# Padding the rows of a scratch array in a long convolution with spectral mixing, with its stores split by partitions

## The chip, the cores and the metric

The kernel runs on one core of a Trainium2 chip. A core has a matrix engine (PE, whose weight loads are listed apart as PEld), a vector engine (DVE), a scalar engine (ACT), a general engine (POOL) and SyncE (SP), which here only issues transfers. Transfers run on 16 DMA engines that all issuing queues share. The metric is the device time in microseconds (us) of one execution. The kernel before took 372.04 us as the median of three runs (370.41 to 372.57).

## The reference

`x` has 8 batches of 5,696 positions and 128 channels. Two stages follow one another: a causal convolution along the positions with a filter `h` as long as the sequence, by an FFT of twice the length, and a spectral mix of the first 64 modes with a small dense layer behind it.

```python
Xf = np.fft.rfft(x, n=2 * S, axis=1)
Hf = np.fft.rfft(h, n=2 * S, axis=0)
x = np.fft.irfft(Xf * Hf[None], n=2 * S, axis=1)[:, :S, :]
X = np.fft.rfft(x, axis=1)
Y[:, :64] = X[:, :64] @ (w_r + 1j * w_i)          # one 128x128 matrix per mode
u = x + np.fft.irfft(Y, n=S, axis=1)
out = u + np.maximum(u @ w_ch, 0.0)
```

The result must have the reference's shape and type (float32); inside, the kernel works in float16 with float32 sums.

## The kernel before

**The tiling.** 5,696 is 64 x 89. The FFT is done by matrix multiplications in two steps, over the 89 and over the 64; there are 90 coarse frequencies `k` (`NK`), and for each of them 64 fine ones, with real and imaginary part. Two batches go through together, as one group; there are four groups, 0 to 3. A group has 23 ticks (`NT`), each with four of the 90 frequencies, the last with two.

**One tick.** PE makes the spectrum of the tick's frequencies (`second`). ACT or DVE reads it from PSUM, and DVE multiplies it with the filter's spectrum (`products`, line 652) into a tile U. The filter's spectrum `h_sb` has two halves: `Hs` as it is cast from PSUM, and a copy with the partitions 0 to 63 and 64 to 127 exchanged. That exchange is made by two DMA copies of 64 partitions, issued by SP (`filter_tick`), once per tick and only while group 0 runs: the first six ticks' copies before the ticks begin, and then tick t makes those of tick t + 6. Two ticks later (`LC` = 2) PE transforms U back over the 64 fine frequencies with the matrices W1 and W2, and ACT casts the two results from PSUM into one of the tiles Zs and Zt (6 of them in the first ticks, later 8 or 10). One tick after that `modes` reads the same tile, to sum the 64 modes that the mix needs.

**Z and its scratch array.** Z doesn't fit into SBUF with all the rest, so each tick stores its tile to the array `zscr` in HBM: partition p = ri x 64 + j (ri is the real or imaginary part, j the position within the 64) with four frequencies of 2 x 128 channels each, 512 bytes in a piece. In the array a row is one (frequency, ri) and holds the 64 j one after the other, 64 x 512 = 32,768 bytes. In the last stage `load_zt` reads chunks of 16 j: 128 rows into one tile (ZT0a to ZT4a) and the remaining 52 into another (ZT0b to ZT4b), 8,192 bytes from each row. Sixteen chunks are read; the first ones begin during the ticks of group 3. PE then finishes the inverse transform from them (`u_z`), adds the mixed modes (`u_c`), and does the dense layer (`o_tile`), whose results SP stores to the output.

**The order of the work.** Everything is put in order by hand. `Recorder` notes each operation with what it reads and writes, and adds semaphore waits; each engine then runs its own list in that order. All DMAs on the SP list are issued one after the other: one that waits, or is slow to issue, holds up those behind it. In tick t of group 0 the list has the Z store of tick t - 2, then the two Hs copies of tick t + 6, and after every other tick up to 11 a load of the table G. Each DMA takes the next semaphore of its ring (`z` for Z stores, 10 of them; `s` for Hs copies, 8), and before a semaphore is used again its former DMA must have landed. The ring `q` has no user.

POOL issues the loads of x for the next group (two DMAs at a time) and of the mix weights. Nearly all operations are recorded by helpers, so the profile names lines of helpers: 320 issues a DMA, 323 a matmul, 311 and 313 are ACT's reads of PSUM, 315 and 317 DVE's.

Of the kernel before, what the change touches and what calls it, by code (L numbers as in the profile page):

```python
# [4 lines left out]
P = 128  # L5
F16 = mybir.dt.float16
# [117 lines left out]
def bass_long_conv_fft__then__afno_spectral_mix_kernel(nc, x, h, moe_w_r, moe_w_i, moe_w_ch, out):  # L124
    B, S, D = x.shape
    M = moe_w_r.shape[0]
    assert D == P and M == 64 and B == 8
    J = 64
# [3 lines left out]
    NK = NQ + 1  # L132
    NP = B // 2
    KT = 4
    NT = (NK + KT - 1) // KT
# [15 lines left out]
    c, s = np.cos(th), np.sin(th)  # L151
# [43 lines left out]
    c_sg = nc.inline_tensor(np.ascontiguousarray(sg.astype(np.float32)), name="cSG")  # L195
    c_g = const("cG", g)
    wd = nc.dram_tensor("wscr", [P, 2 * M * D], F16, kind="Internal")
    zs = nc.dram_tensor("zscr", [NP * NK * P, 2 * D], F16, kind="Internal")


    base = (nc.sbuf_base + 63) // 64 * 64
# [4 lines left out]
    def at(name, cols, dt, off):  # L206
        return nc.alloc_sbuf_tensor_at(name, [P, cols], dt, offset=off)
# [39 lines left out]
    z_s = [at(f"Zs{i}", 1024, F16, a_st + NU * 4096 + (NXS + i) * 2048) for i in range(NZ)] + \  # L247
# [8 lines left out]
    ZB = 16  # L256
    NC = 5
    ZP = ZB * 2 * D
# [5 lines left out]
    zt = [[at(f"ZT{i}{'ab'[p_]}", ZP, F16, zt_off[i][p_]) for p_ in range(2)] for i in range(NC)]  # L264
# [28 lines left out]
        return bass.AP(ps, p0 * 4096 + bank * 512 + off, [[4096, n]] + [list(d) for d in dims])  # L293

    R = Recorder(nc)
    for name, n in (("c", 16), ("x", 26), ("z", 10), ("w", 16), ("t", 20), ("s", 8), ("o", 12), ("p", 16), ("q", 10)):
        R.ring(name, n)

    def bank(i):
        return ("bank", i)  # L300
# [18 lines left out]
    def dma(eng, dst, src, ring, reads=(), writes=(), after=()):  # L319
        R.add(eng, lambda h_: h_.dma_start(dst, src), reads, writes, ring=ring, after=after)  # L320
# [6 lines left out]
    def once(key, toks):  # L327
        if key in first:
            return []
        first[key] = 1  # L330
        return list(toks)
# [3 lines left out]
    def turns(name, items):  # L335
        i = ring2.get(name, 0)
        ring2[name] = i + 1
        return items[i % len(items)]
# [18 lines left out]
    def x_load(g_, i, dst, toks, after=()):  # L357
        b, c_ = divmod(i, XC)
        for p_, (q0, n) in enumerate(((QA, NQ - QA), (0, QA))):
            dma("gpsimd", bass.AP(dst, q0 * XB, [[XB, n], [1, XB]]),  # L360
                bass.AP(x.tensor, x.offset + (2 * g_ + b) * S * D + q0 * J * D + c_ * XB, [[J * D, n], [1, XB]]),
                "x", (), [toks[p_]], after=after)

    def x_place(i, src, toks):
        R.add("vector", lambda e: e.tensor_copy(bass.AP(x_sb, i * XN * XS, [[XW, NQ], [XS, XN], [1, D]]),  # L365
                                                src),
              list(toks) + XZ, [("xin", i)])
# [73 lines left out]
    for j in range(16):  # L441
        t = turns("h", [0, 2, 4])
# [14 lines left out]
        if j % 2:  # L457
            i = j // 2 % 2 * XC + j // 4
# [23 lines left out]
    def xtok(n):  # L482
        return [("xt", n, p_) for p_ in range(2)]

    def x_room(g_, i):
        if g_ > 1:
            return x_st[i]
        return x_h[i] if i < NXH else x_st[i - NXH]
# [41 lines left out]
    def load_zt(i):  # L530
        g_, c_ = divmod(i, J // ZB)
        for part, (p0, r0, n) in enumerate(((0, 0, P), (PB, P, RB))):
            old = list(once(("zt", i % NC, part), zt_old[i % NC][part]))
            dma("sync", bass.AP(zt[i % NC][part], p0 * ZP, [[ZP, n], [1, ZP]]),
                bass.AP(zs, (g_ * 2 * NK + r0) * J * 256 + c_ * ZB * 256, [[J * 256, n], [1, ZP]]),
                "t", [("zd", g_, s_) for s_ in range(NT)], [("zt", i % NC, part)], after=old)

    def clear_zt(i):
        z32 = zt[i][1][0:PB, :].bitcast(U32)
# [44 lines left out]
    def with_h_at(g_, t):  # L584
        return g_ == 0 and t + LH < NT
# [3 lines left out]
    def copied(g_, t, sl):  # L589
        n = len(ticks[t])  # L590
        e = onchip[(g_, t)] = turns("e", list(range(NXS)))
        evac(bass.AP(x_s[e], 0, [[1024, P], [512, 2], [1, n * D]]), pv(sl, 0, [[512, 2], [1, n * D]]), [bank(sl), bank(sl + 1)],
             [("xs", e)], eng="scalar")
        return e

    def twin(g_, t):
        return g_ > 0 and t % 2 == 1

    def straight(g_, t):
        return g_ > 0 and t % 4 == 3  # L600

    def slot_of(g_, t):
        if t == 0:
            return ZSLOT
        if g_ == 0:
            return XSLOT[(t + 1) % 2 if not with_h_at(g_, t) else 0]
        return XSLOT[t % 4 // 2]

    def second(g_, t, d0=0, d1=D, bs=(0, 1)):
        sl = slot_of(g_, t)  # L610
        rd = AST if d1 == D else [("as", j) for j in range(d1 // 4)]
        for i, k in enumerate(ticks[t]):
            for r in range(2):
                for b in bs:
                    col = k * 3 * J + (J if r == 0 else 0) + b * J
                    mm(pv(sl + b, i * D + d0, [[1, d1 - d0]]),
                       ap(m_sb, MW, J * b, J, col, [[1, P]]),
                       ap(a_sb, AW, J * b, J, (2 * k + r) * D + d0, [[1, d1 - d0]]), r == 0, r == 1,
                       rd + mtok(k), [bank(sl + b)])

    def first_u(b, s_, row, tok, d0, d1):
        n = len(ticks[0])
        R.add("vector", lambda e: e.tensor_tensor(  # L623
            bass.AP(u_s[0], b * 512 + d0, [[2048, P], [1024, 2], [D, n], [1, d1 - d0]]),
            bass.AP(s_[0], s_[1] + d0, [[row, P], [0, 2], [D, n], [1, d1 - d0]]),
            bass.AP(h_sb, d0, [[2 * HW, P], [HW, 2], [D, n], [1, d1 - d0]]), MULT),
              [tok, ("h", 0, 0), ("h", 0, 1, 0), ("h", 0, 1, J)], [("u", 0)])
# [36 lines left out]
    def tick(g_, t):  # L664
        if g_ + 1 < NP:
            for i in range(2 * XC):
                if t == XPLACE[g_ > 0][i]:
                    x_place(i, bass.AP(x_room(g_ + 1, i), 0, [[XB, NQ], [D, XN], [1, D]]), xtok(i))
        with_h = with_h_at(g_, t)
        if t < NT:  # L670
            of_two = t > 0 and twin(g_, t - 1)
            if not of_two:
                if straight(g_, t):
                    second(g_, t + 1)
                if t:
                    second(g_, t)
                if t == 1:
                    d_ = DA if g_ else DF
                    second(g_, 0, d_, D, (0,))
                    first_u(0, (ps, slot_of(g_, 0) * 512), 4096, bank(slot_of(g_, 0)), d_, D)  # L680
            products(g_, t, slot_of(g_, t))
            if straight(g_, t):
                copied(g_, t + 1, slot_of(g_, t + 1))
            elif twin(g_, t):
                second(g_, t + 1)
        if g_ + 1 < NP:
            i = t // 2 - 1 if t % 2 == 0 else -1
            if g_ == 0:
                i = XLATE.index(t) + NXH if t in XLATE else -1
            if 0 <= i < 2 * XC:  # L690
                x_load(g_ + 1, i, x_room(g_ + 1, i), xtok(i), [("u", t % NU)] + AST)
        if LC <= t < NT + LC:
            s_ = t - LC
            n = len(ticks[s_])
            i, zi = s_ % NU, zroom(g_, s_)
            zb = [turns("z", ZBANK) for b in range(2)]
            for b in range(2):
                for r in range(2):
                    mm(pv(zb[b], 0, [[1, n * D]]), (W1, W2)[r], u_s[i][:, r * 1024 + b * 512:r * 1024 + b * 512 + n * D],
                       r == 0, r == 1, [("u", i), ("wc",)], [bank(zb[b])])  # L700
                evac(bass.AP(z_s[zi], b * D, [[1024, P], [2 * D, n], [1, D]]),
                     pv(zb[b], 0, [[D, n], [1, D]]), [bank(zb[b])], [("zs", zi, b)], eng="scalar",
                     after=once(("zx", zi, b), Z_OLD) if zi >= NZ else ())
                if b == 0:
                    drained(g_, t, 0)
            zo = (g_ * NK + KT * s_) * P * 256
            dma("sync", bass.AP(zs, zo, [[256, P], [P * 256, n], [1, 256]]),
                bass.AP(z_s[zi], 0, [[1024, P], [256, n], [1, 256]]), "z",
                [("zs", zi, 0), ("zs", zi, 1)], [("zd", g_, s_)])
        drained(g_, t, 1)  # L710
        late = g_ + 1 < NP and t in (NT, NT + 1)
        if late and t > NT:
            modes(g_, t - LM - 1)
            drained(g_, t, 2)
        if LM <= t < NT + LM and not (late and t == NT):
            modes(g_, t - LM)
        if with_h:
            filter_tick(t + LH, [2, 3])
# [126 lines left out]
    for hb in range(2):  # L845
        evac(bass.AP(y_sb, hb * 32 * B, [[2 * M * B, P], [B, 32], [M * B, 2], [1, B]]),
             pv(6 + hb, 0, [[2 * B, 32], [B, 2], [1, B]]), [bank(6 + hb)], [("y", hb)], eng="vector" if hb else "scalar",
             after=ZY)
# [66 lines left out]
    for g_ in range(NP):  # L915
        last = g_ == NP - 1
        order = [(c_, b) for b in range(2) for c_ in range(NCH)] if last else [(c_, b) for c_ in range(NCH) for b in range(2)]
        for n, (c_, b) in enumerate(order):
            i = NCH * g_ + c_
# [46 lines left out]
```

## Time and profile before

| what | value |
|---|---|
| median of three runs | 372.04 us |
| lowest and highest run | 370.41 and 372.57 us |
| span of the profiled execution | 370.1 us |
| ticks of group 0 in it (first product to last) | 43.4 to 88.3 us |
| ticks of group 3 and the first ZT loads | 210 to 262 us |
| last stage | from 256 us |
| Z stores | 92 |
| granted PE clock | 1.00 in all stretches up to 355 us |

The profiled execution is the one that a profiler recorded; its times are counted from its first instruction. "x15" is a number of instructions. In a timeline each row has the start, the length and what ran; rows of the same kind that follow one another closely are merged, and idle time in front is given in brackets with what ended it. Tables by stretch give the busy time of each engine (with the number of instructions), the granted clock, the share of time in which the 16 DMA engines were busy (over 1 where packets overlap) and the bytes per second. A DMA row on SP lasts as long as its issue takes; the time to landing, which is given apart, runs from its issue until the data has arrived.

### The profile page before, as it was taken

The page shows a single profiled execution, that of the slowest core. Times are in us where ns is not written, and L with a number is a line of the kernel's source. Part 1 is how long each engine was busy: PE and PEld are TensorE (multiplying, and loading weights), DVE is VectorE, ACT ScalarE, POOL GpSimd, SP SyncE. Part 2 cuts the span into 40 slices and gives each one's busy share as a digit, 9 for nine tenths or more (in the row PEclk, how much of TensorE's full clock was granted, in tenths as well). Part 3 has the DMA queues.
Part 4 walks back from the last instruction along what each step waited for, and adds up shares of the span by engine and source line. Part 5 has one row for each costly group of instructions (what it writes and reads, how often), then busy time and mean ns, then how long its engine had stood idle before and what let it go on. Part 6 is the DMA issues. An engine that isn't in the chain of part 4 may idle for free.

```text
span 370.1 us, 12455 instructions
## 1 busy us (share of the span) xinstructions
PE 354.7 (96%) x5350; PEld 276.5 (75%) x5350; DVE 291.8 (79%) x332; ACT 316.2 (85%) x499; POOL 75.2 (20%) x117
## 2 busy tenths in 40 slices
PE   7999899999999999999999999999999999999994
PEld 7878766667866668866668766668899888888873
DVE  3549899988999999989999988775357777756666
ACT  8559999999999999999999999995467777688885
POOL 8804012100833311823213001151000000000000
PEclk9999999999999999999999999999999999999999
DMA  7999979969999996999996999999999999999878
GB/s 139 209 271 382 249 165 292 232 198 283 93 140 213 263 258 186 132 160 215 263 278 128 171 310 363 342 345 388 381 410 386 413 410 408 418 399 376 326 291 349
DMA packets 87048, 103.94 MB, mean 281 GB/s; under 512 B 22730, under 2 KB 72522, under 8 KB 83438
## 3 DMA queue, kind: packets, MB, share of 16 engines
q1 hardware_dynamic: 64610, 81.33, 62.5%
q0 software_dynamic: 22384, 21.83, 35.4%
q8 instruction: 42, 0.69, 0.7%
q14 instruction: 12, 0.10, 0.1%
HBM read 70.61 MB, written 51.12 MB: 329 GB/s over the span
## 4 chain that ended last, share of the span: by engine, by line
PE 78%; ACT 10%; DMA 7%; DVE 3%; issue 1%; POOL 1%; DVEq 0%; POOLq 0%
PE ps L323 78%; ACT As L313 6%; DMA out_dram<-O 5%; DMA Hin<-in_h_dram 2%; ACT R L898 1%; DVE As L317 1%; ACT Xs L311 1%; DVE U L623 1%; POOL Hin L320 1%; ACT UT L311 1%; DVE O L899 0%; ACT Zs L311 0%; DVE Hp L438 0%; ACT C L313 0%; DVE Hs L315 0%
## 5 line engine op out<-in xcount | busy, mean ns | idle before, releaser
L652 DVE TENSOR_TENSOR U<-Xs,Hs 128x2048 f16<-128x2048 f16 (+1 forms) x72 | 85.8, 1197 | 12.1 <-ACT Xs L311 11.5
L323 PE MATMUL ps<-U,Wc 128*128 128x512 f16 (+1 forms) x368 | 93.8, 376 | 1.4 <-DVE U L623 1.4
L311 ACT CAST Xs<-ps 128x1024 f16<-128x1024 f32 (+1 forms) x76 | 75.0, 995 | 5.8 <-PE ps L323 3.1
L311 ACT CAST Zs<-ps 128x512 f16<-128x512 f32 (+1 forms) x132 | 70.1, 605 | 0.7
L899 DVE TENSOR_TENSOR O<-ps,R 128x512 f32<-128x512 f32 x81 | 52.4, 684 | 21.6 <-ACT R L898 11.4
L898 ACT ACTIVATE R<-ps 128x512 f32<-128x512 f32 (+1 forms) x92 | 50.5, 592 | 8.5 <-PE ps L323 8.4
L317 DVE TENSOR_SCALAR As<-ps 128x720 f16<-128x720 f32 x64 | 53.1, 879 | 4.8 <-PE ps L323 3.3
L323 PE MATMUL ps<-As,M 64*128 64x128 f16 (+3 forms) x1504 | 52.5, 214 | 2.4 <-ACT As L313 1.2
L313 ACT ACTIVATE As<-ps 128x720 f16<-128x720 f32 (+1 forms) x68 | 48.2, 771 | 5.0 <-PE ps L323 4.8
L323 PE MATMUL ps<-F,Xin 128*128 128x180 f16 x512 | 52.1, 249 | 0.1
L323 PE MATMUL ps<-WI,UT 128*128 128x256 f16 x360 | 50.8, 278 | 0.5 <-ACT UT L311 0.4
L311 ACT CAST UT<-ps 128x712 f16<-128x712 f32 x46 | 34.5, 752 | 19.4 <-PE ps L323 18.4
L323 PEld LDWEIGHTS ps<-U,Wc 128*128 128x128 f16 x368 | 29.1, 97 | 28.2 <-DVE U L623 1.9
L323 PEld LDWEIGHTS ps<-F,Xin 128*128 128x128 f16 x512 | 45.2, 155 | 6.7 <-DVE Xin L365 0.9
L323 PEld LDWEIGHTS ps<-As,M 64*128 64x128 f16 x1504 | 42.2, 94 | 8.7 <-ACT Xs L311 1.9
L323 PEld LDWEIGHTS ps<-WI,UT 128*128 128x128 f16 x360 | 38.9, 152 | 3.2 <-issue 1.8
L323 PE MATMUL ps<-IBs,C 128*128 128x356 f16 x128 | 39.2, 314 | 0.8 <-DVE O L899 0.7
L320 POOL DMA_DIRECT2D Xt<-in_x_dram x40 | 21.4, 540 | 76.5 <-PE ps L323 76.0
L323 PEld LDWEIGHTS ps<-G,Zs 128*128 128x128 f16 x512 | 26.1, 96 | 14.1 <-ACT Zs L311 0.2
L652 DVE TENSOR_TENSOR U<-ps,Hs 128x2048 f16<-128x2048 f32 (+1 forms) x16 | 35.5, 2216 | 0.0
L323 PE MATMUL ps<-G,Zs 128*128 128x128 f16 (+2 forms) x512 | 31.9, 192 | 0.1
L311 ACT CAST Zt<-ps 128x512 f16<-128x512 f32 x52 | 29.1, 659 | 0.0
(76 smaller groups left out, 479.4 us busy)
## 6 DMA issues: line engine op xcount, KB each, us to landing
out_dram<-O SPq DMA_DIRECT2D x39, 512.0 KB, 10.5
zscr<-Zs SPq DMA_DIRECT2D x62, 256.0 KB, 6.7
zscr<-Zt SPq DMA_DIRECT2D x26, 256.0 KB, 6.6
Xt<-in_x_dram POOLq DMA_DIRECT2D x20, 320.0 KB, 6.9
W<-wscr SPq DMA_DIRECT2D x4, 1024.0 KB, 8.5
ZT0a<-zscr SPq DMA_DIRECT2D x4, 1024.0 KB, 11.0
M<-cM POOLq DMA_DIRECT2D x5, 720.0 KB, 17.6
ZT1a<-zscr SPq DMA_DIRECT2D x3, 1024.0 KB, 11.1
```

What stands on the lines that cost most here:

```text
L311: R.add(e, lambda h_: h_.copy(dst, src), reads, writes, after=after)
L313: R.add(e, lambda h_: h_.activation(dst, src, COPY, scale=scale), reads, writes, after=after)
L317: R.add(e, lambda h_: h_.tensor_scalar_mul(dst, src, scale), reads, writes, after=after)
L320: R.add(eng, lambda h_: h_.dma_start(dst, src), reads, writes, ring=ring, after=after)
L323: R.add("tensor", lambda h_: h_.matmul(o, l, r, start=st, stop=sp), reads, writes)
L623: R.add("vector", lambda e: e.tensor_tensor(bass.AP(u_s[0], b * 512 + d0, [[2048, P], [1024, 2], [D, n], [1, d1 - d0]]), bass.AP(s_[0], s_ ...
L652: R.add("vector", lambda e: e.tensor_tensor(uv, src, hv, MULT), bk + [("h", t, 0), ("h", t, 1, 0), ("h", t, 1, J)], [("u", i)])
L898: R.add("scalar", lambda e: e.activation(rv, src_r, RELU), bk, [("r", i % NR)], after=once(("r", i % NR), G_ALL + XTT + [("y", 0), ("y", 1 ...
L899: R.add("vector", lambda e: e.tensor_tensor(ov, src_u, rv, ADD), bk + [("r", i % NR)], [key + (h_,)], after=once(key, old))
```

## The change

A row of `zscr` becomes 34,816 bytes long (64 pieces of 512 bytes and 2,048 bytes that nothing uses). As the rows of the real and imaginary part of one frequency no longer follow one another without a gap, a tick's store becomes two DMAs of 64 partitions each, one per ri, with the same 512-byte pieces. The loads read the same bytes at the new pitch and wait for both stores of each tick. The ring `z` grows from 10 to 16 semaphores, the ring `q` shrinks from 10 to 4.

```diff
-    zs = nc.dram_tensor("zscr", [NP * NK * P, 2 * D], F16, kind="Internal")
+    ZRW = J * 2 * D + 1024
+    zs = nc.dram_tensor("zscr", [NP * NK * 2, ZRW], F16, kind="Internal")
...
-    for name, n in (("c", 16), ("x", 26), ("z", 10), ("w", 16), ("t", 20), ("s", 8), ("o", 12), ("p", 16), ("q", 10)):
+    for name, n in (("c", 16), ("x", 26), ("z", 16), ("w", 16), ("t", 20), ("s", 8), ("o", 12), ("p", 16), ("q", 4)):
...
-                bass.AP(zs, (g_ * 2 * NK + r0) * J * 256 + c_ * ZB * 256, [[J * 256, n], [1, ZP]]),
-                "t", [("zd", g_, s_) for s_ in range(NT)], [("zt", i % NC, part)], after=old)
+                bass.AP(zs, (g_ * 2 * NK + r0) * ZRW + c_ * ZP, [[ZRW, n], [1, ZP]]),
+                "t", [("zd", g_, s_, r) for s_ in range(NT) for r in range(2)], [("zt", i % NC, part)], after=old)
...
-            zo = (g_ * NK + KT * s_) * P * 256
-            dma("sync", bass.AP(zs, zo, [[256, P], [P * 256, n], [1, 256]]),
-                bass.AP(z_s[zi], 0, [[1024, P], [256, n], [1, 256]]), "z",
-                [("zs", zi, 0), ("zs", zi, 1)], [("zd", g_, s_)])
+            for ri in range(2):
+                dma("sync", bass.AP(zs, (2 * (g_ * NK + KT * s_) + ri) * ZRW, [[256, J], [2 * ZRW, n], [1, 256]]),
+                    bass.AP(z_s[zi], ri * J * 1024, [[1024, J], [256, n], [1, 256]]), "z",
+                    [("zs", zi, 0), ("zs", zi, 1)], [("zd", g_, s_, ri)])
```

## The prediction

> **What bounds the kernel now.** I read the page first, for the engines and the chain of waits.
>
> ```profile
> span 370.1 us, 12455 instructions
> ...
> PE 354.7 (96%) x5350; PEld 276.5 (75%) x5350; DVE 291.8 (79%) x332; ACT 316.2 (85%) x499; POOL 75.2 (20%) x117
> ...
> PE 78%; ACT 10%; DMA 7%; DVE 3%; issue 1%; POOL 1%; DVEq 0%; POOLq 0%
> ```
>
> PE is busy for 354.7 of 370.1 us, and the chain that ended last is PE for 78%. No Z transfer is named on it. So the change can take away little: at most some of the 15 us in which PE stands, and most of those are the start and the tail. It can add wherever a transfer that PE or DVE needs becomes late. The question is therefore how close each of SP's transfers is to being late. I looked at the tables by stretch, and then at SP's own timeline in the group that runs with the filter (group 0).
>
> ```profile
> 50.00:62.00 12.00, 12.00 (x246) 7.92 (x240) 11.99 (x15) 11.36 (x18) 2.32 (x4) 1.00 0.98 226
> 62.00:74.00 12.00, 12.00 (x258) 8.09 (x257) 11.67 (x15) 11.46 (x18) 2.07 (x4) 1.00 1.06 248
> 74.00:86.00 12.00, 11.99 (x202) 7.66 (x199) 9.84 (x11) 11.83 (x20) 0.00 (x0) 1.00 0.72 206
> ```
>
> Columns: length, busy PE, PEld, DVE, ACT, POOL, clock, DMA share, GB/s. PE loses nothing from 50 to 86 us: every delay there is new time. SP isn't in that table; its timeline is (start, length, what):
>
> ```profile
> 50.31 0.46 SPq L320 DMA_DIRECT2D zscr<-Zs  x1
> ...
> 69.88 2.04 SPq L320 DMA_DIRECT2D Hs<-Hs  x2
> 71.96 0.59 SPq L320 DMA_DIRECT2D zscr<-Zs  x1
> 72.64 1.22 SPq L320 DMA_DIRECT2D Hs<-Hs  x2
> 73.91 0.60 SPq L320 DMA_DIRECT2D zscr<-Zs  x1
> 74.61 1.45 SPq L320 DMA_DIRECT2D Hs<-Hs  x2
> 76.10 1.20 SPq L320 DMA_DIRECT2D zscr<-Zs  x1
> 77.41 1.10 SPq L320 DMA_DIRECT2D Hs<-Hs  x2
> 78.94 0.36 SPq L320 DMA_DIRECT2D zscr<-Zs  x1
> ...
> 80.59 1.91 SPq L320 DMA_DIRECT2D zscr<-Zs  x1
> 82.60 1.11 SPq L320 DMA_DIRECT2D Hs<-Hs  x2
> ...
> 84.44 1.14 SPq L320 DMA_DIRECT2D Hs<-Hs  x2
> 85.62 1.76 SPq L320 DMA_DIRECT2D zscr<-Zs  x3
> 87.42 2.48 SPq L320 DMA_DIRECT2D zscr<-Zt  x4
> ```
>
> Each row begins some 0.1 us after the one above ends. The only real hole is 0.43 us, before 78.94. SP issues without a rest for 35 us: it is **full**, though nothing on the page says so, since SP has no busy row. In each tick it issues one Z store and one pair of Hs copies, and DVE's product needs that pair:
>
> ```profile
> 77.68 0.41 DVE L315 CAST Hs<-ps 128x256 f16<-128x256 f32 x1
> ...
> 78.62 1.21 DVE L652 TENSOR_TENSOR U<-Xs,Hs 128x2048 f16<-128x2048 f16 x1
> ...
> 87.61 0.69 DVE L652 TENSOR_TENSOR U<-Xs,Hs 128x1024 f16<-128x1024 f16 x1 [0.24 <-ACT Xs L311]
> ```
> ```profile
> zscr<-Zs SPq DMA_DIRECT2D x16, 256.0 KB, 5.0
> Hs<-Hs SPq DMA_DIRECT2D x28, 64.0 KB, 5.2
> ...
> Hs<-Hs SPq DMA_DIRECT2D x2, 32.0 KB, 1.9
> ```
>
> The last tick (22) has two frequencies, so its H is cast at 77.68 (128x256), its copies are the pair of 32 KB, and its product is the 128x1024 one at 87.61. H was ready at 78.09, and SP issued the pair at 84.44: SP is 6.35 us behind. The second copy goes out at about 84.44 + 1.14 - 0.60 = 84.98 and lands 1.9 later, at 86.9: 0.7 us before the product. Five ticks earlier (the pair at 72.64, its second copy at about 73.26) the median landing of 5.2 gives 78.5, for the product at 78.62. Nobody waits for Hs today, by less than a microsecond.
>
> **The change part by part.** *The second store.* The 92 Z stores become 184, all on SP, with the same bytes in the same 512-byte pieces. What does one more issue cost? Three whole stores in a row take 1.76 (0.59 each), four take 2.48 (0.62 each), two Hs copies, which also have 64 partitions and only 64 pieces, 1.14 (0.57 each). So an issue in a full queue costs about 0.57 to 0.62 whatever it moves; I take 0.60.
>
> In group 0 tick t issues the Z store of tick t-2 and then the Hs pair of tick t+6. Ahead of the pair of tick 22 stand the stores of ticks 0 to 14: 15 more issues, 15 x 0.60 = 9.0 us. Subtract the 0.7 of slack and the 0.4 hole: 7.9 us late, if all else on SP stays as it is. It may not. From 50.31 to 85.58 SP spends 35.3 us on 15 stores, 15 pairs and two G loads. At 0.59 a store, 1.12 a pair, 0.14 for the gaps of a tick and 0.64 a G load this would be 15 x 1.85 + 1.3 = 29.1. The other 5.8 us, less the 0.4 hole 5.4, are long issues (2.04, 1.20, 1.91). Some fall on POOL's issues of x loads:
>
> ```profile
> 51.52 1.03 POOL L320 DMA_DIRECT2D Xt<-in_x_dram  x2 [19.76 <-PE ps L323]
> ...
> 69.90 1.04 POOL L320 DMA_DIRECT2D Xt<-in_x_dram  x2 [4.95 <-PE ps L323]
> ```
>
> If the long issues only mean that the transfer engines were full (share 0.98 and 1.06), a slower SP would lose them, and the delay is 7.9 - 5.4 = 2.5. If all stay it is 7.9. Two of the longest stand after 74 us, where the share is 0.72, and the x loads stay, so I keep two thirds: **+6.1 us, between 2.5 and 7.9**. The product is late, then DVE, PE behind it and every later group; no stage has idle time to win it back.
>
> *Groups 1 and 2* cost nothing: SP has no Hs copies there, and mostly waits for the data.
>
> ```profile
> SPq L320 <- ACT Zs L311: 33.0, 14, 16.0
> ```
> ```profile
> L320 SPq DMA_DIRECT2D zscr<-Zs x15: 359/360/1582, 106.6 to 143.1; - x15
> ```
>
> 17 us of waiting behind the first store (33.0 less the longest, 16.0) against 23 issues of 0.36 (8.3 us). Without that cover they'd cost the same 0.6 each.
>
> *Group 3* is full again, with the first ZT loads between the stores:
>
> ```profile
> 239.45 1.81 SPq L320 DMA_DIRECT2D zscr<-Zs  x2
> ...
> 251.47 0.66 SPq L320 DMA_DIRECT2D ZT2a<-zscr  x1
> 252.17 2.37 SPq L320 DMA_DIRECT2D ZT2b<-zscr  x1
> ```
> ```profile
> PEld ps L323 <- DMA ZT2b<-zscr: 0.3, 1, 0.3
> ```
> ```profile
> 245.00:262.00 17.00, 16.13 (x324) 13.63 (x322) 9.14 (x10) 10.41 (x16) 4.95 (x5) 1.00 1.04 377
> ```
>
> PE already waits 0.3 us for ZT2b, so this load has no slack. Seven stores (ticks 13 to 19) stand between 239.45 and 251.47: seven more issues at 0.36 to 0.60 are 2.5 to 4.2 us. But the DMA share is 1.04 there and issues last 2.4 us: SP is held by full transfer engines, and an issue added to that costs nothing while they stay full. Bounds 0 and 4.2; I take 1.0.
>
> *The new pitch* could speed up loads and stores. Z loads alone (262 to 275 us) move 408 GB/s:
>
> ```profile
> DMA packets 998, 5.30 MB, mean 408 GB/s; under 512 B 104, under 2 KB 370, under 8 KB 370
> ```
> ```profile
> 280.00:300.00 20.00, 20.00 (x287) 17.88 (x285) 14.88 (x23) 14.56 (x25) 0.00 (x0) 1.00 1.02 407
> ```
>
> With output stores among them (280 to 300 us) it is 407: the old pitch isn't slower than other traffic, and PE is busy for 20.00 of 20. I take 0 for the pitch; bounds -0.6 (the wait of 0.3 for ZT2b, and one more like it) and 0.
>
> The Trainium skill (DMA: Bandwidth & Descriptors, Latency and other measured facts) tells to pad a pitch that is a large power of two: 512 KiB gives 207 GB/s, a padded one 214. By this rule 32 KiB could gain a few per cent of the loads; the row of 408 GB/s leaves little room for it. The same page (Issuing engines are not separate DMA queues) calls the sequencer's time to issue "usually small relative to the DMA itself"; by that the second store would be free and the sum 372.0. The 0.59 of an issue is small beside a landing of 5.0, as it says, but it is SP's 35 full microseconds that count here.
>
> *The rings.* Ring z has 16 slots for two stores a tick, 8 ticks instead of 10. Z buffers are reused after 6 to 10 ticks, so this waits for nothing new; ring q is not used. ACT now has two store semaphores to wait for before it refills a Z buffer; in group 0 they are late by the same SP delay as Hs, not one more.
>
> *Sum.* 6.1 + 0 + 1.0 + 0 = 7.1 us. The profiled execution spans 370.1; the median of the runs is 372.04, 1.9 us above it. 370.1 + 7.1 = 377.2 profiled, **379.1 us** as a median.
>
> **The rivals.** *A, an issue costs by its pieces.* If half a store took half the issue time, two halves would cost SP what one did, Hs would be as early as now, and the median stay at 372.0 (371.4 with the 0.6 of the pitch): not slower. It decides if halves show 0.30 in the full stretch. Against it: a copy of 64 pieces takes 0.57, a store of 512 pieces 0.59.
>
> *B, the long issues go.* SP's stretches vanish, +2.5 in group 0 and 0 in group 3: 374.5. For it: share 1.06 from 62 to 74 us. Against: 1.91 and 1.20 where the share is 0.72.
>
> *C, 64 partitions move slower.* From 107 to 144 us, in group 1, the two DMA queues take, of 16 engines:
>
> ```profile
> q1 hardware_dynamic: 11349, 5.64, 51.8%
> q0 software_dynamic: 1097, 2.93, 49.2%
> ```
>
> The engines are full there, and 51.8% of 37 us are 19.2 us for 23 stores, 0.83 each. If a store in two halves took a quarter more, 0.21 x 23 = 4.8 us in each of groups 1 and 2 would have no room: 379.1 + 9.6 = 388.7. For it: nothing in the trace shows a store of 64 partitions. Against: Hs copies, which have 64, land in 1.9.
>
> *D, the pitch helps more than I see,* in loads, stores and Hs behind them. The gain is capped by PE's stops between the start and the tail:
>
> ```profile
> 42.00:355.00 313.00, 306.97 (x4817) 235.52 (x4818) 256.04 (x288) 275.19 (x447) 55.09 (x79) 1.00 1.00 283
> ```
>
> 6.0 us in all; half of them would give 369. Against: neither Hs nor, but for 0.3 us, a ZT load costs PE anything now.
>
> **How the numbers follow.** My forecast (SP late by 4 to 12 us in all) 0.62, B 0.13, C 0.08, A 0.11, D 0.06. A change within 0.5% (370.2 to 373.9) can't be told from none. Faster: D, 0.06. Same: A, and of B's low end a little: 0.12. Slower: 0.82. The range goes from 373.2 (between A and B) to 386: 2.5 to 7.9 in group 0 with 0 to 4.2 in group 3 give 374.5 to 384.1, and part of C.
>
> **What would show it.** In the changed profile SP should have no holes from 50 to about 92 us, with second halves of about 0.6; DVE's products of ticks 13 to 22 should wait for Hs<-Hs; the product of 128x1024 should start near 94 instead of 87.6; groups 1 and 2 should keep their length; the wait for ZT2b should grow to about 1 us. I am wrong if halves issue in 0.3, if Hs pairs stay as early as now, or if groups 1 and 2 grow.

## The result, and the profile after

| | before | changed |
|---|---|---|
| median of four runs | 371.88 us | 381.77 us |
| lowest and highest run | 370.41 and 372.57 us | 380.28 and 387.2 us |
| ratio | | 1.025, 95% interval 1.0205 to 1.0294 |
| span of the profiled execution | 370.1 us | 378.4 us |

The changed kernel is slower. Its run of 387.2 us counts as a slow one; ratios leave such runs out, here and below, and medians keep them (without it 380.87 us). The profiled execution is the fastest run, 380.28 us. One line was added above the helpers, so lines 311 to 323 and 652 of before are 312 to 324 and 653 now. From the page of the changed kernel, its totals, the chain that ended last, and the Z stores:

```profile
span 378.4 us, 12581 instructions
...
PE 355.9 (94%) x5350; PEld 275.9 (73%) x5350; DVE 291.6 (77%) x332; ACT 316.8 (84%) x499; POOL 75.9 (20%) x117
...
PE 74%; ACT 11%; DMA 6%; DVE 5%; issue 2%; SPq 1%; POOL 1%; DVEq 0%; ACTq 0%; POOLq 0%
...
zscr<-Zs SPq DMA_DIRECT2D x124, 128.0 KB, 5.9
```

PE has the same 5,350 matmuls and is busy 1.2 us more (354.7 before). So nearly all the new time is time in which PE stands. The page doesn't say where; a table of stage lengths does. A group is counted from the start of its first DVE product to the start of its last, the last stage from the first use of a ZT0 tile to the end (us, worked out from the timelines):

| | group 0 | group 1 | group 2 | group 3 | last stage | span |
|---|---|---|---|---|---|---|
| before | 44.19 | 38.35 | 38.37 | 37.71 | 121.26 | 370.06 |
| changed | 54.36 | 38.36 | 38.43 | 37.70 | 119.98 | 378.44 |

Group 0 grew by 10.17 us. Groups 1, 2 and 3 grew by less than 0.1 each. The last stage is 1.28 shorter, and the rest of the span 0.57 shorter. 10.17 + 0.06 - 1.28 - 0.57 = 8.4, the difference of the spans.

The table by stretch of the changed kernel (length, busy PE, PEld, DVE, ACT, POOL with their instructions, clock, DMA share, GB/s) covers group 0, four of its microseconds alone, and group 1:

```profile
50.00:62.00 12.00, 11.94 (x250) 7.90 (x249) 11.99 (x16) 11.36 (x19) 2.31 (x4) 1.00 0.89 182
62.00:74.00 12.00, 8.89 (x186) 5.38 (x180) 7.93 (x10) 8.04 (x14) 1.33 (x3) 1.00 0.86 207
74.00:86.00 12.00, 9.34 (x181) 6.14 (x174) 8.61 (x11) 8.47 (x14) 0.74 (x2) 0.91 0.76 172
86.00:98.00 12.00, 11.01 (x136) 6.57 (x132) 6.32 (x7) 10.17 (x17) 0.00 (x0) 0.94 0.51 129
82.00:86.00 4.00, 3.20 (x49) 2.12 (x50) 3.69 (x6) 2.97 (x5) 0.00 (x0) 0.74 0.57 149
114.00:151.00 37.00, 36.53 (x564) 23.68 (x564) 35.33 (x32) 36.08 (x60) 8.33 (x16) 1.00 1.16 233
```

Before, PE was busy for all of 50 to 86 us at clock 1.00. Now it stands for 3.11, 2.66 and 0.99 us in the three stretches from 62 to 98, and the clock of the last two is 0.91 and 0.94, which is another 12 x (0.09 + 0.06) = 1.8 us of full speed: 8.6 together, most of the 10.17. The DMA share fell in each stretch up to 74 us (0.89 and 0.86, from 0.98 and 1.06): the transfer engines are not what is full. Four rows of SP's timeline show what is (start, length, what; x2 is two issues):

```profile
84.20 1.28 SPq L321 DMA_DIRECT2D zscr<-Zs  x2
85.57 1.21 SPq L321 DMA_DIRECT2D Hs<-Hs  x2
86.83 2.62 SPq L321 DMA_DIRECT2D zscr<-Zs  x2
...
94.83 1.21 SPq L321 DMA_DIRECT2D Hs<-Hs  x2
```

Two halves take 1.28 us, where a whole store took 0.59. A tick without a long issue lasts from 84.20 to 86.83, 2.63; before, it lasted from 83.75 to 85.62, 1.87. So a second store costs SP 0.76 per tick, and the row of 2.62 shows that long issues are still there. SP gets from the first Z store of group 0 to the end of tick 22's Hs pair in 35.27 us before (50.31 to 85.58) and in 46.21 now (49.83 to 96.04): 10.94 more for 15 more issues, 0.73 each. Who waits for this is in the view of the waits of the changed kernel from 50 to 98 us (total, times, longest), and on DVE's timeline, where the wait stands in brackets:

```profile
DVE U L653 <- DMA Hs<-Hs: 9.4, 6, 3.1
...
ACT Zs L312 <- DMA zscr<-Zs: 6.4, 3, 2.8
...
PE ps L324 <- DVE Hs L316: 4.3, 4, 2.7
```
```profile
80.91 1.23 DVE L653 TENSOR_TENSOR U<-Xs,Hs 128x2048 f16<-128x2048 f16 x1 [3.08 <-DMA Hs<-Hs]
...
84.19 0.42 DVE L316 CAST Hs<-ps 128x256 f16<-128x256 f32 x1
...
97.52 0.69 DVE L653 TENSOR_TENSOR U<-Xs,Hs 128x1024 f16<-128x1024 f16 x1 [1.26 <-DMA Hs<-Hs]
```

Neither the wait for Hs nor that for zscr was in this view before. DVE waits for the copies in six products (those of ticks 10, 12, 15, 16, 20 and 22), and ACT for Z stores that have not landed and still hold the Z buffers. PE then waits for DVE. Tick 22's H is ready at 84.61, and SP issues its pair at 94.83: SP is 10.2 us behind, where it was 6.35. The last product of the group starts at 97.52 instead of 87.61, and all later work is late by about as much.

### The profile page after: what moved, and what is told of

Same layout as the page of the kernel before. It is cut to its first block, busy times and chain, and to the rows that moved or that the text cites. A ratio compares the mean times of both kernels' runs of the same rounds, so it can differ in the third digit from the quotient of the medians.

```text
span 378.4 us, 12581 instructions
## 1 busy us (share of the span) xinstructions
PE 355.9 (94%) x5350; PEld 275.9 (73%) x5350; DVE 291.6 (77%) x332; ACT 316.8 (84%) x499; POOL 75.9 (20%) x117
## 4 chain that ended last, share of the span: by engine, by line
PE 74%; ACT 11%; DMA 6%; DVE 5%; issue 2%; SPq 1%; POOL 1%; DVEq 0%; ACTq 0%; POOLq 0%
PE ps L324 73%; ACT As L314 6%; ACT Xs L312 2%; DMA Hs<-Hs 2%; DMA Hin<-in_h_dram 2%; DMA zscr<-Zs 2%; DVE As L318 1%; ACT R L899 1%; SPq L321 1%; DVE U L653 1%; ACT Zs L312 1%; DVE U L624 1%; POOL Hin L321 1%; DVE Hs L316 1%; DVE Hp L439 0%
## 5 line engine op out<-in xcount | busy, mean ns | idle before, releaser
L653 DVE TENSOR_TENSOR U<-Xs,Hs 128x2048 f16<-128x2048 f16 (+1 forms) x72 | 85.8, 1197 | 22.3 <-ACT Xs L312 11.1
L324 PE MATMUL ps<-U,Wc 128*128 128x512 f16 (+1 forms) x368 | 95.0, 379 | 4.2 <-ACT Zs L312 1.5
L653 DVE TENSOR_TENSOR U<-ps,Hs 128x2048 f16<-128x2048 f32 (+1 forms) x16 | 35.5, 2216 | 0.0
L312 ACT CAST Zt<-ps 128x512 f16<-128x512 f32 x52 | 29.1, 645 | 1.1 <-PE ps L324 1.1
```

The costliest lines, as they stand in the source:

```text
L312: R.add(e, lambda h_: h_.copy(dst, src), reads, writes, after=after)
L324: R.add("tensor", lambda h_: h_.matmul(o, l, r, start=st, stop=sp), reads, writes)
L653: R.add("vector", lambda e: e.tensor_tensor(uv, src, hv, MULT), bk + [("h", t, 0), ("h", t, 1, 0), ("h", t, 1, J)], [("u", i)])
```

## The experiments

Three theories stood against one another. **S**: the loss is SP's list in group 0, which is full and gets 15 more issues ahead of tick 22's copies. **P**: it is the pitch. **T**: transfers of 64 partitions move slower or crowd the transfer engines. Each ratio is against the kernel before on the same chip, with its 95% interval. The line numbers of the helpers and of the products move by a few lines with the edits (L652, L653 and L657 are the same product).

### One part of the change at a time

Three kernels keep the old pitch and split the store in all groups (e1_split_old_pitch), in group 0 alone (e4_split_group0) and in groups 1 to 3 alone (e5_split_groups123). All three have 16 semaphores in ring z and 4 in ring q. The edit against before, for e4; e1 has 2 throughout, e5 has `g_ > 0`:

```diff
...
-            dma("sync", bass.AP(zs, zo, [[256, P], [P * 256, n], [1, 256]]),
...
+            for ri in range(2 if g_ == 0 else 1):
+                np_ = J if g_ == 0 else P
+                dma("sync", bass.AP(zs, zo + ri * J * 256, [[256, np_], [P * 256, n], [1, 256]]),
...
```

The fourth (e2_pitch_one_store) has a new pitch and one store: the two rows of a frequency stay together, and 2,048 bytes stand behind each pair.

```diff
+    ZK = 2 * J * 2 * D + 1024
+    zs = nc.dram_tensor("zscr", [NP * NK, ZK], F16, kind="Internal")
...
+            dma("sync", bass.AP(zs, zo, [[256, P], [ZK, n], [1, 256]]),
...
```

> The stores are split as in the change, the pitch stays 32,768 bytes. Theory S (SP's full queue in group 0 takes the time): group 0 as long as in the changed kernel (54.4 us from first to last product, 44.2 before), time 380 to 383. Theory P (the pitch takes it): group 0 at 44 to 45 us, time 371 to 373.

> The pitch alone: a frequency's pair of rows takes 65,536 + 2,048 bytes, so one store of 128 partitions per tick still does. Theory S: group 0 at 44.2 us as before, time 370.5 to 372.5; if the 1.3 us that the last stage is shorter in the changed kernel (120.0 against 121.3 us) come from the pitch, they show here, 370.6. Theory P: 380 or more.

> Split stores in group 0 alone, old pitch. Theory S: the whole loss, 380 to 383, group 0 at 54 us. Theory T (a transfer of 64 partitions is slower, in whatever group): a part of it, in proportion some 374.

> Split stores in groups 1 to 3 alone, old pitch. Theory S: SP has room there, 371 to 373, group 0 at 44 us. Theory T: most of the loss, 378 or so. If the order of group 3's loads suffers from seven more issues, the first use of ZT1 to ZT4 comes 1 to 4 us later against that of ZT0.

| | median us | ratio | group 0 | last stage |
|---|---|---|---|---|
| e1, split in all groups | 384.31 | 1.0282 (1.0211 to 1.0353) | 53.08 | 124.06 |
| e4, split in group 0 | 381.40 | 1.0224 (1.0173 to 1.0274) | 54.16 | 119.89 |
| e5, split in groups 1 to 3 | 374.89 | 1.0043 (1.0011 to 1.0074) | 46.36 | 121.44 |
| e2, pitch, one store | 372.21 | 0.9987 (0.996 to 1.0014) | 45.25 | 120.65 |

The split alone makes the whole loss; the pitch alone makes none. That refutes P. e1 lies 1.3 us above its range of 380 to 383: its group 0 is no longer than that of the changed kernel, but its last stage is. The split in group 0 alone loses as much as the change, within the intervals, and its waits from 50 to 98 us are of the same two kinds:

```profile
DVE U L652 <- DMA Hs<-Hs: 7.6, 5, 2.1
...
ACT Zs L311 <- DMA zscr<-Zs: 6.8, 4, 2.1
```

Nor does the pitch bring anything. In e2's table by stretch, the loads alone (262 to 275 us) move 383 GB/s, and with output stores among them (280 to 300) 400; before had 408 and 407. So a longer pair of rows moved nothing faster:

```profile
262.00:275.00 13.00, 12.73 (x226) 11.25 (x224) 5.08 (x6) 6.25 (x9) 0.00 (x0) 1.00 0.98 383
280.00:300.00 20.00, 20.00 (x286) 17.87 (x285) 14.64 (x23) 14.50 (x25) 0.00 (x0) 1.00 1.01 400
```

e2 spaces pairs of rows, 67,584 bytes apart, where the change spaces single rows, so it isn't the very same pitch; but e4 has the old one and as short a last stage as the change (119.89 and 119.98), so the 1.28 us that the last stage lost are no gain of the pitch. That stage varies from 119.9 to 124.1 among the kernels. Part of what moves it is in PE's waits in e1 from 260 to 288 us:

```profile
PE ps L323 <- DMA ZT2a<-zscr: 1.7, 1, 1.7
PE ps L323 <- DMA ZT2b<-zscr: 0.9, 1, 0.9
```

For these two loads, issued during group 3, PE waits 2.6 us in e1, and in the later kernels 2.4 in e11 and 2.3 in e7, but not at all in the changed kernel and in e4. e7 doesn't split the stores of group 3, so such a wait needs no further issues there. The rest of what moves the last stage stays open.

e5 is a small miss: S gave it no loss, and it shows 0.4%. In its profiled execution groups 1, 2 and 3 take 38.38, 38.51 and 37.72 us, as before. The excess is in group 0 (46.36 against 44.19), whose stores e5 doesn't split. There SP's timeline and the waits from 50 to 92 us read:

```profile
76.12 2.19 SPq L320 DMA_DIRECT2D Hs<-Hs  x2
...
85.76 1.13 SPq L320 DMA_DIRECT2D Hs<-Hs  x2
```
```profile
DVE U L652 <- DMA Hs<-Hs: 1.3, 2, 0.7
```

Long issues brought tick 22's pair to 85.76 instead of 84.44, more than the 0.7 of slack, and two products waited. This shows how close group 0 stands to the edge. e2, whose list has no further issue either, crosses it too in its profiled execution (1.9 us of waits for Hs). Why e5 crosses it more often than before does isn't known.

### Issues without the bytes

Is it the issue or the half store? In e6_tiny_each_tick the kernel before gets, behind each Z store of group 0, a transfer of 512 bytes in 16 pieces. It writes an array that nothing reads; the computation and the Z stores are those of before. e7_tiny_every_second adds it for even ticks only, e14_tiny_late for the stores of ticks 7 to 14.

```diff
...
+            if g_ == 0:
+                dma("sync", bass.AP(xs_d, s_ * 256, [[16, 16], [1, 16]]), bass.AP(f1_sb, 0, [[2 * NK, 16], [1, 16]]), "q",
+                    [("f1",)], [("xd", s_)])
```

> The kernel before, with one more DMA of 512 bytes (16 pieces of 32) on SP behind each Z store of group 0, into an array that nothing reads. Theory S (the number of issues on SP counts): group 0 near 53 to 54 us, time 379 to 383, as with the split. Theory T (what the halves move counts): group 0 near 44 us, 371 to 373.

> The same, behind every second Z store only: half the dose, 8 issues of 0.60 ahead of tick 22's copies. Theory S: 4.8 us less some 1 us of slack, 375 to 377.5. If SP's queue only jams from some load on: 372. Theory T: 371 to 373.

> The kernel before with the 512-byte DMA behind the stores of ticks 7 to 14 alone: 8 issues, as many as behind every second store, but after most of the x loads. Theory S by issues alone: 8 x 0.7 less 0.7 to 1, 376 to 377.5. A theory in which the half dose cost 6.9 us because early issues meet the x loads and PE's clock falls in the stop: less than with every second store, 374 to 376.5, with the clock at 1.00.

| | issues ahead of tick 22's pair | median us | ratio | group 0 |
|---|---|---|---|---|
| e6 | 15 | 379.73 | 1.0183 (1.0129 to 1.0236) | 52.21 |
| e7 | 8 | 378.90 | 1.0162 (1.0107 to 1.0218) | 51.30 |
| e14 | 8 | 376.02 | 1.0098 (1.0065 to 1.0132) | 47.64 |

e6 has most of the loss of e4 (7.7 us over its before, against 8.8) with 512 bytes in place of half a store. That speaks against T and against a price by pieces. SP's timeline in e6:

```profile
89.45 0.58 SPq L321 DMA_DIRECT2D zscr<-Zs  x1
90.08 0.53 SPq L321 DMA_DIRECT2D xscr<-F  x1
90.70 1.11 SPq L321 DMA_DIRECT2D Hs<-Hs  x2
91.85 0.59 SPq L321 DMA_DIRECT2D zscr<-Zs  x1
```

Sixteen pieces of 32 bytes take 0.53 us to issue, 512 pieces of 512 bytes 0.58. A tick lasts 91.85 - 89.45 = 2.40, which is 0.53 more than before.

e7 misses its range of 375 to 377.5. Half the issues cost nearly as much as all. SP explains a part: it reaches the end of tick 22's pair 5.26 us later than before (40.53 against 35.27), which less the slack of 0.7 makes 4.6, while group 0 grew by 7.1. The rest is in e7's table by stretch and at one product of DVE:

```profile
74.00:78.00 4.00, 3.73 (x70) 2.29 (x64) 1.49 (x2) 3.31 (x5) 0.00 (x0) 1.00 0.82 135
78.00:82.00 4.00, 1.13 (x24) 0.98 (x24) 3.02 (x4) 1.07 (x2) 0.00 (x0) 0.77 0.91 273
82.00:86.00 4.00, 4.00 (x34) 2.12 (x31) 2.10 (x3) 2.66 (x4) 0.00 (x0) 0.50 0.66 188
86.00:90.00 4.00, 4.00 (x56) 2.33 (x55) 2.03 (x2) 3.52 (x7) 0.00 (x0) 0.88 0.64 179
```
```profile
78.98 1.23 DVE L653 TENSOR_TENSOR U<-Xs,Hs 128x2048 f16<-128x2048 f16 x1 [3.50 <-DMA Hs<-Hs]
```

One wait of 3.50 us left PE busy for 1.13 of 4 us: PE stood for 3.14 us, until 80.87. In the next 4 us PE is busy all the time, at clock 0.50. The slow clock comes to 4 x (0.23 + 0.50 + 0.12) = 3.4 us of full speed, of which some 0.4 passed while PE still stood (the clock is 0.57 from 80 to 81, where PE is busy for 0.13). 4.6 + 3.0 = 7.6 is somewhat more than the 7.1 measured, so part of the slow clock must have lain beside the lateness. The Trainium skill (TensorE: Matmul & The Clock Gate, Why this matters for your kernels) says to keep PE-idle gaps between bursts below about 3 us, because one idle window brings the clock back to 4/8; this trace agrees, with 0.50 behind a stop of that length. But the clock also fell behind shorter ones, of 2.66 us in the changed kernel, 2.44 in e6 (0.64 from 82 to 86 us), 2.31 in e13 (0.58 there) and 1.69 in e11 (0.83 from 267 to 277 us), and not behind those of 2.28 in e8 and 2.27 in e7's last stage (1.00 in both), so these runs show no sharp limit at 3 us.

e14 has as many issues ahead of tick 22's pair as e7, without such a stop. Its table by stretch and its wait from 50 to 98 us:

```profile
62.00:74.00 12.00, 12.00 (x259) 8.03 (x251) 11.62 (x15) 11.40 (x18) 2.07 (x4) 1.00 1.07 260
74.00:86.00 12.00, 11.76 (x195) 7.22 (x194) 8.45 (x10) 11.01 (x19) 0.00 (x0) 1.00 0.56 156
86.00:98.00 12.00, 9.97 (x117) 7.90 (x115) 9.07 (x11) 9.87 (x18) 1.26 (x2) 1.00 0.75 220
```
```profile
DVE U L653 <- DMA Hs<-Hs: 2.6, 2, 2.2
```

PE has no stop as long as 1.5 us, the clock stays at 1.00, the waits for Hs are 2.6 us, and group 0 grows by 3.5, half of e7's. Its 376.02 lies in both ranges that were expected, so it doesn't measure the clock's share by itself; it agrees with 8 issues costing about 4 us as long as PE never stops for long.

### The same bytes from another queue

In e11_second_half_pool the changed kernel's second halves in group 0 are issued by POOL. Transfers, bytes, pieces and pitch are those of the change; ring q has 6 semaphores, ring z 14.

```diff
...
-                dma("sync", bass.AP(zs, (2 * (g_ * NK + KT * s_) + ri) * ZRW, [[256, J], [2 * ZRW, n], [1, 256]]),
-                    bass.AP(z_s[zi], ri * J * 1024, [[1024, J], [256, n], [1, 256]]), "z",
+                dma("gpsimd" if ri and g_ == 0 else "sync", bass.AP(zs, (2 * (g_ * NK + KT * s_) + ri) * ZRW, [[256, J], [2 * ZRW, n], [1, 256]]),
+                    bass.AP(z_s[zi], ri * J * 1024, [[1024, J], [256, n], [1, 256]]), "q" if ri and g_ == 0 else "z",
```

> The changed kernel with the second half of each store of group 0 issued by POOL (ring q of 6, ring z of 14): as many transfers with the same bytes, but SP issues three DMAs per tick as before the change. Theory S: group 0 at 44 to 47 us, 371.5 to 375. Theory T (more or smaller transfers on the shared engines take the time, whoever issues them): group 0 stays above 52 us, 379 or more.

376.14 us (374.15 to 378.75), 1.0102 (1.0054 to 1.0149): above the range's end, yet the loss fell from 9.9 to 4.1 us, and group 0 from 54.36 to 46.76. Of the 5.3 us by which its profiled execution exceeds before's, 2.6 are in group 0 and 2.6 in the last stage, with the wait for ZT2a and ZT2b. SP's timeline, the waits from 50 to 98 us:

```profile
84.53 0.62 SPq L321 DMA_DIRECT2D zscr<-Zs  x1
85.24 1.20 SPq L321 DMA_DIRECT2D Hs<-Hs  x2
86.49 0.62 SPq L321 DMA_DIRECT2D zscr<-Zs  x1
```
```profile
DVE U L653 <- DMA Hs<-Hs: 3.0, 2, 2.3
...
ACT Zs L312 <- DMA zscr<-Zs: 1.4, 1, 1.4
```

A tick on SP lasts 1.96 us, close to before's 1.87, and a store of 64 partitions alone takes 0.62, as much as one of 128. So the queue that issues decides, and not the transfer: T expected over 52 us.

What e11 still loses in group 0 is on SP's list as well. The table has, worked out from SP's timelines in us, how much more than in before (35.27) passes from the first Z store of group 0 to the end of tick 22's pair, the same less the slack of 0.7, and what group 0 grew by:

| | changed | e4 | e1 | e6 | e14 | e11 | e7 |
|---|---|---|---|---|---|---|---|
| SP later | 10.9 | 11.0 | 10.1 | 9.0 | 4.6 | 3.4 | 5.3 |
| less the slack | 10.2 | 10.3 | 9.4 | 8.3 | 3.9 | 2.7 | 4.6 |
| group 0 longer | 10.2 | 10.0 | 8.9 | 8.0 | 3.5 | 2.6 | 7.1 |

Only e7, with its slow clock, is off by more than some 0.5 us. e11 has as many issues there as before; its 15 ticks are 0.09 longer each, and its long issues, as what each takes beyond 0.65 us, come to 6.7 instead of 5.0. That is 3.0 of the 3.4. The Trainium skill (DMA: Bandwidth & Descriptors, Rules for kernel authors) advises against splitting a transfer into two disjoint halves of the partitions, because both use the same 16 engines; no run here gained from the split, but most of what it cost is not on those engines, as e11 has the same halves on them.

### Fewer copies, and another order

If SP's number of issues decides, copies made once for two ticks should pay for the second stores. In e8_after_wide_hs the changed kernel makes the Hs pairs of ticks 8 to 21 once per two ticks, with the odd one; e10_before_wide_hs does so in the kernel before, and e12_pitch_wide_hs is e2 with the same, the likeliest candidate to beat before. In e13_copies_first the changed kernel's Hs pair goes ahead of the tick's stores.

```diff
-        for p0, p1 in ((0, J), (J, 0)):
+        two = t > LH + 1 and t < NT - 1
+        lo = lo - KT * D if two else lo
+        for p0, p1 in ((0, J), (J, 0)) if not two or t % 2 else ():
...
```

> The changed kernel with the Hs copies of ticks 8 to 21 made by one pair for two ticks, issued with the odd tick: SP has 2 store issues and 1 copy issue per tick in group 0, three as before the change. Theory S: the loss goes, 371 to 374, group 0 at 44 to 46 us. A theory in which the Z stores themselves land too late for their buffers, whatever SP does: 378 or more, with ACT Zs waiting for zscr.

> The kernel before with the same wide copies: SP has 2 issues per tick in place of 3. Theory S: SP has room, but nothing waited for it in the kernel before, so 370.5 to 372.5; at most the 1 us by which group 0 differs from run to run is won.

> The candidate: the kernel before with the padded pitch in one store per tick and the wide Hs copies. Theory S: SP has room and nothing gains from it, 370.5 to 372.5. A theory in which the kernel before already loses a little to SP in group 0 and to the pitch in the last stage: 369.5 to 370.5.

> The changed kernel with the two Hs copies of a tick ahead of its two stores on SP. Theory S (the number of issues in the queue counts): the backlog is the same but for one pair of stores, 379 to 382; DVE waits less for Hs, ACT more for the Z buffers. A theory in which only the order behind the stores hurts: 372 to 375.

| | median us | ratio | group 0 |
|---|---|---|---|
| e8, changed, wide copies | 377.80 | 1.0141 (1.0081 to 1.0201) | 48.66 |
| e10, before, wide copies | 371.69 | 0.998 (0.9952 to 1.0007) | not given |
| e12, e2, wide copies | 372.24 | 1.0005 (0.9977 to 1.0034) | 45.27 |
| e13, changed, copies first | 384.31 | 1.031 (1.0268 to 1.0352) | 53.90 |

(e10's profiled execution is its longest run, 376.32 us.)

e8 got less back than expected: it is above its range of 371 to 374, with a ratio of 1.0141 against the change's 1.025. With 14 issues fewer on SP's list than in the changed kernel, group 0 still grows by 4.5 us over before. SP takes 38.55 us to the end of tick 22's pair, 3.3 more than before, and an even tick's copies go out a tick later, behind four stores; what each of the two takes isn't separated. From e8's SP timeline, and its wait for Hs from 40 to 105 us:

```profile
79.12 1.53 SPq L321 DMA_DIRECT2D Hs<-Hs  x2
80.70 2.63 SPq L321 DMA_DIRECT2D zscr<-Zs  x4
83.37 2.48 SPq L321 DMA_DIRECT2D Hs<-Hs  x2
```
```profile
DVE U L657 <- DMA Hs<-Hs: 5.6, 3, 3.1
```

In e10 and e12 the fewer issues gain nothing, as PE has nothing to win there: no version that I ran beats the kernel before.

In e13 the wait only changes place. It is 2.3 us above its range of 379 to 382; group 0 agrees with S, and what it lost beyond that is in group 1 (39.84 us) and the last stage. Its waits from 50 to 98 us:

```profile
ACT Zs L312 <- DMA zscr<-Zs: 8.8, 5, 2.9
...
DVE U L653 <- DMA Hs<-Hs: 5.2, 4, 1.6
```

DVE waits less for the copies (5.2 from 9.4), ACT more for its Z buffers (8.8 from 6.4), and group 0 is nearly as long as in the changed kernel (53.90 and 54.36). Here the full list costs the same whichever of its transfers goes first.

## Why the prediction was right

It gave 379.1 us, the time is 381.77. The mechanism is shown; the term of group 0 was too small, that of group 3 too large. The sum was made for the profiled execution, and there the terms missed in both directions: 377.2 forecast, plus 4.1 in group 0, less 1.0 in group 3, less 1.3 in the last stage and 0.6 elsewhere, is the 378.4 measured. That it came so close is partly luck. The median lies another 1.5 us above the profiled run.

**SP's list is the bound of group 0.** Right: one hole of 0.5 us from 50 to 96 us, second halves of 0.62, products waiting for Hs (9.4 us in all, in six of the ticks from 10 on), and groups 1 and 2 unchanged. The last product came at 97.5, where the forecast had 94. e4 puts the loss in group 0, e11 puts it on the issuing queue, e6 on the issue itself.

**The price of an issue, 0.60, was too low.** It left out what a tick pays around the second issue: two halves take 1.28, not 1.19, and the Hs pair behind them 1.21 instead of 1.14. Rows of a tick without long issues give 0.76; the mean over 15 is 0.73. This makes 10.9 instead of 9.0.

**"I keep two thirds" of the long issues was wrong.** Its subtraction has a slip: 35.3 less 29.1 is 6.2, not 5.8, so the long issues would be 5.8 after the hole, the lower bound 2.1 and the term 6.0. Summed over the issues as what each took beyond 0.65 us, they are 5.0 us before and 4.5 after: nearly all stayed. With 10.94 less the slack of 0.7, and the 0.4 of the hole not taken off, since each list has one hole of that size (0.43 and 0.50 us), the term is 10.2, which is what group 0 grew by (10.17). The step's +6.1 lay 4.1 us too low, and even its bound of 7.9 was passed.

**Group 3's +1.0 was 0 in the profiled execution.** The length of group 3 is the same to 0.01 us. ZT2b, which the prediction gave no slack, is issued at 263.1, and its first matmul starts at 272.1 without a wait for it. Counted from the first product of group 3, the issue is 1.2 us later than before (45.0 and 43.7) and the matmul 0.2 earlier (54.0 and 54.2). In the view of that tile in the changed kernel (instructions; duration in ns; first and last start):

```profile
L324 PE MATMUL ps<-S4b,ZT2b x96: 203/204/207, 272.1 to 351.8; 84*128 84x89 f16 x96
L321 SPq DMA_DIRECT2D ZT2b<-zscr x3: 401/408/414, 263.1 to 308.9; - x3
```

So the seven issues made SP 1.2 us later there, not 2.5 to 4.2, and PE lost nothing: the lower bound of that term. That is one execution and not a rule, as e1, with the same seven issues, waited 2.6 us for ZT2a and ZT2b.

**Groups 1 and 2, and the pitch, at 0.** Both right, by the stage table and by e2. The rule of the Trainium skill (DMA: Bandwidth & Descriptors, Latency and other measured facts) on padding a large power of two brings nothing at this pitch: 383 and 400 GB/s in e2, 408 and 407 before. The prediction set two of its figures side by side that don't belong together: the 214 is for a padded pitch of 4 MiB, so they promise nothing for 32 KiB. The same page's "usually small" for the time to issue (Issuing engines are not separate DMA queues) holds beside a landing of 5.9 us and misleads for the sum, as 0.73 us, 15 times over, is the loss.

**The rings.** "Waits for nothing new" holds for the ring of semaphores, as SP's list shows no hole for it. ACT does wait, 6.4 us in all, for Z buffers, of which 6 are in use in the first twelve ticks of group 0. "Late by the same SP delay as Hs, not one more" was right: e13 moves the wait from the one to the other, and the length of group 0 stays.

**The rivals.** A, a price by pieces, falls with 1.28 for two halves. B falls with the long issues that stayed. C falls with groups 1 and 2, which keep their length with 23 split stores each, and with e11. D falls with e2, and with e1 and e4, which lose as much at the old pitch; a gain smaller than their intervals can't be excluded.

## What to carry to other kernels

Before a transfer is split, read the timeline of the queue that issues it and count issues, not bytes: where rows follow one another without holes, each further issue makes everything behind it late by its full price. That held in group 0. In group 3, where the transfer engines were full (share 1.04) and issues lasted up to 2.4 us already, seven more made the queue only 1.2 us later. Then look for the first reader behind that queue, and at how little slack it has; here, moving one transfer ahead of another only passed the delay on, and another issuer took most of it away. A stop of PE can cost more than its length: here the clock fell behind each of the four longest stops between the start and the tail, of 2.31 to 3.14 us.

## What had not been expected of the hardware

The clock's fall behind a single stop: 0.50 for 4 us and 0.88 for the next 4 in e7, 0.74 from 82 to 86 us in the changed kernel, where the profile before had 1.00 in every stretch up to 355 us. It is a good part of why 8 tiny transfers spread over group 0 cost 6.9 us of the median, nearly as much as 15 (7.7). The mean clock of whole executions goes the same way: 0.990 to 0.995 in e7's four runs, 0.997 to 0.999 in all but one of e14's nine. What decides behind which stop it falls isn't shown.
